# Attention softmax on one core: the exponentials' scale and VectorE's factor read from SBUF columns instead of constants

## The chip, the core and the metric

The kernel runs on one core of one Trainium2 chip. A core has a matrix engine (TensorE, "PE" in the profile; its weight loads are "PEld"), VectorE ("DVE"), ScalarE ("ACT"), GpSimd ("POOL") and a queue for transfers, SyncE ("SP"). They run side by side and meet at semaphores. The on-chip memories are SBUF, with 128 partitions, and PSUM, into which TensorE writes its results.

The metric is the device time of one execution in microseconds (us); smaller is better.

## What is computed

Attention over 32 heads with 2048 rows of 20 columns each, on normalised queries and keys, with one temperature for each head:

```python
def reference(q, k, v, t):
    eps = 1e-6
    qn = q / (jnp.sqrt((q * q).sum(axis=-1, keepdims=True)) + eps)
    kn = k / (jnp.sqrt((k * k).sum(axis=-1, keepdims=True)) + eps)
    logits = jnp.einsum('bhqd,bhkd->bhqk', qn, kn) * t[None, :, None, None]
    attn = _softmax(logits, axis=-1)
    return jnp.einsum('bhqk,bhkd->bhqd', attn, v)
```

The inputs are bf16 with B = 1, H = 32, S = 2048 and D = 640 / 32 = 20. The scores are bounded by the temperature, so the kernel takes no maximum away before the exponential. The sum of the weights comes out of the second product, from a column of ones beside v.

## The kernel before

For each head the 2048 x 2048 scores are cut into units of 128 keys by 512 queries. A unit's scores are one TensorE matmul (`qk_mm`, L837) of the transposed keys with the transposed queries, into a 512-column stretch of PSUM. Four such units side by side make a group, whose product with v (`pv_mm`, L857) is four matmuls that add into the PSUM tile `psO`.

Between the two products each score must become its exponential, and two engines share this work:

- **ScalarE** takes most of the units, in waves of two and three by turns (`WAVES`, `add_wave`, L905). A wave is one activation (L938) over 1024 or 1536 columns: it reads the scores in `psA`, takes the exponential and writes bf16 into the ring `p_ring`. `psA` has room for one wave of each size, so a wave's matmuls wait for the exponential two waves back.
- **VectorE** takes between 3 and 7 of a head's 16 groups (`DVE_TILES`, `add_dgroup`, L964). It reads the scores in `psD` (L998; called a read of scores below), multiplies them by `X_MUL`, adds `X_ADD` and writes int16 into `xt`. Read as a float16 number, that integer is an approximate exponential. Three shifted copies of it (L1008 on VectorE, or in pieces L1012 on GpSimd) and the plain one are each multiplied with a scaled v, and their sum averages the approximation's error. A read covers 1024 columns, or, where a group is in `SPLIT`, 512.

VectorE also prepares the heads to come: squares (L689), sums (L693), the inverse root (L697 to L718), the normalised rows (L735) and the scaled copies of v (L652). It finishes the heads that are done: transpose of `psO` (L870), reciprocal (L879) and product (L887). SyncE's queue loads q, k and v, transposes them by transfers and stores the results.

The order of the work on each engine is computed when the program is built. Each piece of work is a task with an engine, a planned duration, the tasks that it depends on and a priority. `list_schedule` (L118) plays these through time and writes down the order in which each engine takes them; it also chooses the form of the scores' matmuls and cuts GpSimd's pieces to fit beside VectorE's reads. `plan_waits` (L409) then turns the dependences into semaphore waits. A wait is left out where the engine is already known to have seen that count, directly or through a task that it waited for (L441 to L449). `emit` (L454) writes the instructions out. No order is changed while the kernel runs.

At the start VectorE fills constant tiles with memsets (L549), among them the task `z_one`, which fills `ones` with 1.0. TensorE's warm-up matmuls and GpSimd's identity matrix wait for it.

The scale of one other activation is a column in SBUF already: `qt0` (L776) multiplies the first head's queries by `t_f32[:, 0:1]`.

Of the kernel before, what the change touches and what calls it, by code (L numbers as in the profile page):

```python
# [12 lines left out]
F32 = mybir.dt.float32  # L13
# [3 lines left out]
ACT = mybir.ActivationFunctionType  # L17
# [12 lines left out]
X_MUL = 1024.0 * LOG2E  # L30
X_ADD = 1024.0 * (15.0 + math.log2(KEXP))
# [18 lines left out]
class Program:  # L50
# [31 lines left out]
    def add(self, eng, name, fn, dur, deps=(), pri=0.0, lat=0.0, dma=None):  # L82
        t = Task(eng, name, fn, dur, deps, pri, lat, dma)
        self.tasks.append(t)
        return t
# [379 lines left out]
def bass_standalone__qk_norm__prompt_kernel(  # L465
# [11 lines left out]
    WAVES = (2, 3)  # L477
# [27 lines left out]
    EXP0 = 0.063  # L505
# [4 lines left out]
    with ExitStack() as es:  # L510
# [6 lines left out]
        ones = sbuf("ones", [128, 512], BF16)  # L517
        ident = sbuf("ident", [128, 128], BF16)
        nil = sbuf("nil", [128, 32], BF16)
        qk_sb = sbuf("qk_sb", [128, NB * 2 * R, D], BF16)  # L520
        v_all = sbuf("vaug", [128, NV, R, 32], BF16)
        vaug = [v_all[:, i, :, :] for i in range(NV)]
# [25 lines left out]
        def memset(eng, ap, val, dur, pri):  # L548
            return add(eng, "z", lambda e, tk: e.memset(ap, val), dur, pri=pri)  # L549
# [38 lines left out]
        add("ACT", "warm", lambda e, tk: e.activation(act_scr[:, :], act_scr[:, :], ACT.Exp), 1.5, [scr0], -95)  # L588
        ld_t = dma("SP", "ld_t", tb16[:, :], bass.AP(t.tensor, 0, [[0, 128], [1, H]]), [], -40, "t")
        z_nil = memset("POOL", nil[:, :], 0.0, 0.1, -71)  # L590
        z_one = memset("DVE", ones[:, :], 1.0, 0.2, -99)
        z_lib = add("POOL", "lib", lambda e, tk: e.int64_add(
            ident[:, 0:4].bitcast(I64), ident[:, 4:8].bitcast(I64), 0), 0.2, [memset("POOL", ident[:, 4:8], 0.0, 0.1, -99.5)], -99.4)
        z_id = add("POOL", "id", lambda e, tk: e.affine_select(
# [310 lines left out]
        def add_wave(w):  # L905
            us = waves[w]
            slot = w % 2
            hs = sorted({A_units[i][0] for i in us})
            pair = next(([i, i + 1] for i in range(len(us) - 1)
                                          if A_units[us[i]][2] // 2 != A_units[us[i + 1]][2] // 2), [])  # L910
            parts = pair + [i for i in range(len(us)) if i not in pair]

            def f_qk(eng, rows):
                last = None
                for i in parts:
                    h, r, g = A_units[us[i]]
                    last = qk_mm(eng, h, r, g, psA[:, (slot * WAVES[0] + i) * 512:(slot * WAVES[0] + i + 1) * 512], rows)
                return last
            deps = [act.get(w - 2)]
            for h in hs:  # L920
                deps += qk_deps([A_units[u] for u in us if A_units[u][0] == h], w < EARLY_W)
            qk = add("PE", f"q3A{w}", lambda e, tk: f_qk(e, tk.rows), PE_MM, deps, w - 10000.0)
            if len(us) == 3 and LIGHT3:
                qk.modes = [("q3", 32, PE_MM + 0.01, 384.0), ("q2", 64, PE_MM * 2, 768.0)]
            elif len(us) == 3:
                qk.modes = [("q2", 64, PE_MM * 2, 768.0), ("qk", 128, PE_MM * 3, 1536.0)]
            else:
                qk.modes = [("q2", 64, PE_MM, 256.0 * len(us)), ("qk", 128, PE_MM * len(us), 512.0 * len(us)),
                            ("q3", 32, PE_MM, 128.0 * len(us))]
            if w < EARLY_W:  # L930
                qk.modes, qk.rows, qk.dur, qk.work = None, 32, PE_MM + 0.01, 128.0 * len(us)
            qks = [qk]
            for h in hs:
                qk_users[h] += qks
            p0 = us[0] % NP
            n = len(us) * 512
            war = [pv_of_group[(u - NP) // 4] for u in us if u >= NP]
            act[w] = add("ACT", f"exp{w}", lambda e, tk: e.activation(  # L938
                p_ring[:, p0 * 512:p0 * 512 + n], psA[:, slot * WAVES[0] * 512:slot * WAVES[0] * 512 + n], ACT.Exp),
                EXP0 + n / 1200.0, qks + war, w)  # L940

        def add_group(i):
            us = list(range(4 * i, 4 * i + 4))
# [20 lines left out]
        def add_dgroup(jg):  # L964
            js = D_groups[jg]
            sx = se = 0
            ox, oe = place(0, NX, len(js)), place(1, NE, len(js))
            bx, be = 2048 * ox, 2048 * oe
            w = 2048 * len(js)
            old = lambda n, i: last_use.get((n, (ox if n == "x" else oe) + i), [])  # L970
            new = {}
            t1s = []
            for i, j in enumerate(js):
                h, rg = D_tiles[j]
                due = h + (j - d0[h] + 0.3) / DVE_TILES[h] - DLEAD
                split = j in SPLIT
                for us in ((0, 1), (2,), (3,)) if split else ((0, 1), (2, 3)):
                    gs = [GORD[k] for k in us]
                    banks = [k % 2 for k in us]

                    def f_qk(eng, rows, h=h, rg=rg, gs=gs, banks=banks):
                        last = None
                        for g, bk in zip(gs, banks):
                            last = qk_mm(eng, h, rg[g], g, psD[:, 512 * bk:512 * bk + 512], rows)
                        return last
                    deps = [bank_t1.get(bk) for bk in banks] + (q0 if j < EARLY_D else [])
                    for g in gs:
                        deps += qk_deps([(h, rg[g], g)], j < EARLY_D)
                    qk = add("PE", f"qkD{j}.{us[0]}", lambda e, tk, f=f_qk: f(e, tk.rows), PE_MM, deps, due - 20000.0)
                    qk.modes = [("q2", 64, PE_MM, 256.0 * len(us)), ("qk", 128, PE_MM * len(us), 512.0 * len(us)),  # L990
                                ("q3", 32, PE_MM, 128.0 * len(us))]
                    if j < EARLY_D:
                        qk.modes, qk.rows, qk.dur, qk.work = None, 32, PE_MM + 0.01, 128.0 * len(us)
                    qk_users[h].append(qk)
                    for k0, m in [(k, 1) for k in us] if split else [(us[0], 2)]:
                        o = bx + 2048 * i + 512 * k0
                        c = 512 * (k0 % 2)
                        u = add("DVE", f"t1.{j}.{k0}", lambda e, tk, o=o, c=c, w=512 * m: e.tensor_scalar(  # L998
                            xt[sx][:, o:o + w], psD[:, c:c + w], X_MUL, X_ADD, ALU.mult, ALU.add),
                            0.067 + 512 * m / 960.0, [qk] + old("x", i), due - 5)  # L1000
                        for bk in range(k0 % 2, k0 % 2 + m):
                            bank_t1[bk] = u
                        t1s.append(u)
                t1_of[j] = t1s[-(4 if split else 2):]
            sh = []
            for i in range(len(PHASES)):
                dst, w = ss[i][0], 2048 * len(js)
                f = add("DVE", f"s{i}.{js[0]}", lambda e, tk, i=i, dst=dst: e.tensor_scalar(  # L1008
                    dst[:, be:be + w], xt[0][:, bx:bx + w], float(PHASES[i]), None, ALU.add), 0.068 + w / 3840.0,
                    t1s + [u for m in range(len(js)) for u in old(f"s{i}", m)], due)  # L1010
                if len(js) == 1 and jg >= 2:
                    f.alt = lambda c, n, i=i, dst=dst: lambda e, tk: e.int64_add(  # L1012
                        dst[:, be + 2 * c:be + 2 * (c + n)].bitcast(I64), xt[0][:, bx + 2 * c:bx + 2 * (c + n)].bitcast(I64),
                        PHASES[i] * LANES)
                    if chained.get(i) and ox and oe:
                        chained[i].next = f
                    chained[i] = f
                sh.append([(list(range(len(js))), f)])
            for m in range(len(js)):
                new["x", ox + m] = [u for us in sh for ms, u in us if m in ms]  # L1020
            for i, j in enumerate(js):
                h, rg = D_tiles[j]
                for nm, tile, dep, ph in [("x", xt[sx], t1_of[j], None)] + [
                        (f"s{n}", ss[n][se], [u for ms, u in sh[n] if i in ms], n) for n in range(len(PHASES))]:
                    p = add("PE", f"pv{nm}{j}", lambda e, tk, h=h, rg=rg, o=2048 * i + (bx if ph is None else be), tile=tile, ph=ph: pv_mm(
                        e, h, lambda g: rg[g],
                        lambda g: tile[:, o + 512 * GORD[g]:o + 512 * GORD[g] + 512].bitcast(FP16), ph),
                        PE_MM, dep + pv_base(h) + (vsc[h] if ph is not None else []), due + 0.2)
                    p.head = h
                    pv_users[h].append(p)  # L1030
                    new.setdefault((nm, (ox if nm == "x" else oe) + i), []).append(p)
            last_use.update(new)
# [76 lines left out]
```

## Time and profile before

| | us |
|---|---|
| median of 2 runs | 637.17 |
| the runs | 637.06 and 637.29 |
| the profiled execution | 638.55 |
| its span, first to last instruction | 636.8 |

The profile is of one execution. A line of its table of groups names the kernel's line, the engine, the operation, the tile written and the tile read with their shapes, and the count; then the group's busy time in us and the mean duration of one in ns; and last the engine's idle time just ahead of the group with what ended most of it. A line of the timeline begins with the start and the duration in us. A line of the windows view begins with the stretch and its length; then come the busy time of the asked instructions with their count, the granted TensorE clock (1.00 is full), the transfers' share and GB/s.

What belongs to the engines beside it:

| engine | busy us | share of the span | instructions |
|---|---|---|---|
| TensorE | 596.2 | 94% | 6267 |
| VectorE | 627.2 | 99% | 926 |
| ScalarE | 626.0 | 98% | 558 |
| GpSimd | 423.4 | 66% | 461 |

The granted TensorE clock was 1.000 over the span.

### The profile page before, as it was taken

How to read it: one execution, taken by the hardware profiler on the slowest of the kernel's cores; microseconds unless marked ns; L12 is line 12 of the kernel's file. 1: busy time of each engine (PE TensorE's matmuls, PEld its weight loads, DVE VectorE, ACT ScalarE, POOL GpSimd, SP SyncE). 2: the span in 40 equal slices, each digit the busy share in tenths (PEclk: the TensorE clock that was granted, in tenths of full speed). 3: DMA queues.
4: the chain of work that ended last, by engine and by line, in shares of the span. 5: the costliest groups of instructions: out<-in, count | busy, mean ns of one | idle time of the engine just before them, and what ended most of it. 6: DMA issues, size and time to landing. Idle time of an engine off the chain costs nothing.

```text
span 636.8 us, 15281 instructions
## 1 busy us (share of the span) xinstructions
PE 596.2 (94%) x6267; PEld 170.9 (27%) x6267; DVE 627.2 (99%) x926; ACT 626.0 (98%) x558; POOL 423.4 (66%) x461
## 2 busy tenths in 40 slices
PE   8898899999999989999999999999999999999997
PEld 2222222222222222222222222222222222222222
DVE  8999999999999999999999999999999999999997
ACT  7999999999999999999999999999999999999997
POOL 4265687777756787567776675777787777577443
PEclk9999999999999999999999999999999999999999
DMA  4554444333333313333323333433332241321100
GB/s 66 76 78 71 74 85 65 73 58 55 58 59 63 65 45 53 64 67 61 60 59 58 45 66 72 55 61 40 62 64 64 44 69 35 67 50 26 38 1 16
DMA packets 196917, 36.40 MB, mean 57 GB/s; under 512 B 172656, under 2 KB 196848, under 8 KB 196848
## 3 DMA queue, kind: packets, MB, share of 16 engines
q1 hardware_dynamic: 196656, 35.32, 33.3%
q8 instruction: 49, 0.80, 0.6%
q14 instruction: 20, 0.16, 0.1%
q10 hardware_dynamic: 192, 0.11, 0.1%
HBM read 7.87 MB, written 2.62 MB: 16 GB/s over the span
## 4 chain that ended last, share of the span: by engine, by line
ACT 88%; DVE 7%; PE 5%; issue 0%
ACT p_ring L938 88%; DVE xt L998 3%; PE psO L857 2%; DVE ss L1008 1%; PE psA L837 1%; PE psO L760 1%; PE psD L837 1%; DVE rs_sum L693 0%; DVE oT L870 0%; PE psO L802 0%; DVE sq L689 0%; DVE qkn L735 0%; DVE o_stage L887 0%; DVE vph L652 0%; DVE ones L549 0%
## 5 line engine op out<-in xcount | busy, mean ns | idle before, releaser
L938 ACT ACTIVATE p_ring<-psA 128x1024 bf16<-128x1024 f32 (+1 forms) x551 | 622.5, 1429 | 2.3 <-PE psA L837 2.3
L1012 POOL INT64_ADD ss<-xt x430 | 416.1, 972 | 200.3 <-DVE xt L998 51.9
L998 DVE TENSOR_SCALAR xt<-psD 128x1024 int16<-128x1024 f32 (+1 forms) x412 | 414.0, 1021 | 2.4 <-PE psD L837 1.8
L857 PE MATMUL psO<-ss,vph 128*32 128x512 f16 x2016 | 175.6, 385 | 0.0
L1008 DVE TENSOR_SCALAR ss<-xt 128x2048 int16<-128x2048 int16 x182 | 124.9, 688 | 0.6
L857 PE MATMUL psO<-p_ring,vaug 128*32 128x512 bf16 x1376 | 120.7, 384 | 0.0
L837 PE MATMUL psA<-qkT,kR 32*128 32x512 bf16 x619 | 109.4, 384 | 11.6 <-ACT p_ring L938 10.7
L837 PE MATMUL psA<-qz,kR 64*128 64x512 bf16 (+1 forms) x413 | 101.6, 385 | 5.6 <-ACT p_ring L938 5.1
L837 PE MATMUL psD<-qz,kR 64*128 64x512 bf16 (+1 forms) x359 | 97.7, 384 | 7.1 <-DVE xt L998 4.9
L837 PE MATMUL psA<-qkT 32*128 32x512 bf16 x220 | 67.1, 384 | 4.6 <-ACT p_ring L938 4.3
L857 PE MATMUL psO<-xt,vaug 128*32 128x512 f16 x672 | 66.5, 386 | 0.0
L857 PEld LDWEIGHTS psO<-ss,vph 128*32 128x32 f16 x2016 | 44.6, 94 | 74.6 <-issue 59.9
L837 PE MATMUL psD<-qz,qkT 64*128 64x512 bf16 (+1 forms) x123 | 46.5, 384 | 2.0 <-DVE xt L998 1.8
L837 PEld LDWEIGHTS psA<-qkT,kR 32*128 32x128 bf16 x619 | 26.3, 91 | 75.4 <-ACT p_ring L938 73.3
L857 PEld LDWEIGHTS psO<-p_ring,vaug 128*32 128x32 bf16 x1376 | 32.0, 94 | 52.3 <-issue 43.7
L837 PE MATMUL psA<-qz,qkT 64*128 64x512 bf16 (+1 forms) x124 | 43.2, 385 | 0.6 <-ACT p_ring L938 0.4
L837 PEld LDWEIGHTS psA<-qz,kR 64*128 64x128 bf16 (+1 forms) x413 | 24.4, 93 | 65.9 <-ACT p_ring L938 63.6
L837 PE MATMUL psD<-qkT,kR 32*128 32x512 bf16 x145 | 37.7, 382 | 3.2 <-DVE xt L998 2.3
L837 PEld LDWEIGHTS psD<-qz,kR 64*128 64x128 bf16 (+1 forms) x359 | 23.9, 93 | 57.9 <-DVE xt L998 50.4
L857 PEld LDWEIGHTS psO<-xt,vaug 128*32 128x32 bf16 x672 | 17.4, 94 | 31.0 <-issue 24.6
L735 DVE TENSOR_TENSOR qkn<-qk_sb,rs_r 128x640 bf16<-128x640 bf16 x31 | 25.3, 816 | 0.0
L693 DVE TENSOR_REDUCE rs_sum<-sq 128x32 f32<-128x640 bf16 x31 | 25.1, 810 | 0.0
(61 smaller groups left out, 201.0 us busy)
## 6 DMA issues: line engine op xcount, KB each, us to landing
kR<-qkT SPq DMA_DIRECT2D x62, 96.0 KB, 2.1
qz<-qkT SPq DMA_DIRECT2D x127, 32.0 KB, 1.8
kR<-qkT SPq DMA_DIRECT2D x62, 64.0 KB, 2.0
qk_sb<-in_k_dram SPq DMA_DIRECT2D x32, 80.0 KB, 3.0
vaug<-in_v_dram SPq DMA_DIRECT2D x32, 80.0 KB, 3.2
qk_sb<-in_q_dram SPq DMA_DIRECT2D x124, 20.0 KB, 2.5
out_dram<-o_stage SPq DMA_DIRECT2D x31, 80.0 KB, 1.9
kR<-qkT SPq DMA_DIRECT2D x62, 32.0 KB, 1.9
```

Source lines behind the costliest of these rows:

```text
L693: sums.append(dv("sum", lambda e, tk, i=i, k=k, src=src: e.tensor_reduce(rs["sum"][:, 2 * R * (i + k):2 * R * (i + k + 1)], src[:, 2 * R * ...
L735: norm[h] = [dv("norm", lambda e, tk, x=x, b=b, i=i: e.tensor_tensor(qkn[b][:, :, 0:D], x[:, :, :], bc(rs["r"][:, 2 * R * i:2 * R * (i + 1 ...
L760: warm.append(add("PE", "warm", lambda e, tk: e.matmul(psO[:, :], ones[:, 0:128], ones[:, :], start=True, stop=True), PE_MM, [z_one], -300))
L837: return eng.matmul(dst, lhsT, mov, tile_position=(p0, 0))
L857: last = eng.matmul(psO[32 * g:32 * g + 32, :], w, rhs_of(g), start=start, stop=False, skip_group_check=True, tile_position=(0, 32 * g))
L938: act[w] = add("ACT", f"exp{w}", lambda e, tk: e.activation(p_ring[:, p0 * 512:p0 * 512 + n], psA[:, slot * WAVES[0] * 512:slot * WAVES[0] ...
L998: u = add("DVE", f"t1.{j}.{k0}", lambda e, tk, o=o, c=c, w=512 * m: e.tensor_scalar(xt[sx][:, o:o + w], psD[:, c:c + w], X_MUL, X_ADD, ALU ...
L1008: f = add("DVE", f"s{i}.{js[0]}", lambda e, tk, i=i, dst=dst: e.tensor_scalar(dst[:, be:be + w], xt[0][:, bx:bx + w], float(PHASES[i]), No ...
L1012: f.alt = lambda c, n, i=i, dst=dst: lambda e, tk: e.int64_add(dst[:, be + 2 * c:be + 2 * (c + n)].bitcast(I64), xt[0][:, bx + 2 * c:bx + ...
```

## The change

A new tile `cols` of 128 x 2 float32 numbers lies in SBUF. Its first column is filled with 1.0 and its second with `X_MUL` by two memsets, in the same task as the memset of `ones` and ahead of it. Every exponential takes its scale from the first column, where before it had the constant 1.0. Every read of scores takes its factor from the second, where before it had the constant `X_MUL`; the addend `X_ADD` stays a constant. Both kinds of task now also depend on `z_one`. The numbers computed with are the same.

```diff
+        cols = sbuf("cols", [128, 2], F32)
...
-        z_one = memset("DVE", ones[:, :], 1.0, 0.2, -99)
+        z_one = add("DVE", "z", lambda e, tk: (e.memset(cols[:, 0:1], 1.0), e.memset(cols[:, 1:2], X_MUL),
+                                               e.memset(ones[:, :], 1.0))[2], 0.2, pri=-99)
...
             act[w] = add("ACT", f"exp{w}", lambda e, tk: e.activation(
-                p_ring[:, p0 * 512:p0 * 512 + n], psA[:, slot * WAVES[0] * 512:slot * WAVES[0] * 512 + n], ACT.Exp),
-                EXP0 + n / 1200.0, qks + war, w)
+                p_ring[:, p0 * 512:p0 * 512 + n], psA[:, slot * WAVES[0] * 512:slot * WAVES[0] * 512 + n], ACT.Exp, scale=cols[:, 0:1]),
+                EXP0 + n / 1200.0, qks + war + [z_one], w)
...
                         u = add("DVE", f"t1.{j}.{k0}", lambda e, tk, o=o, c=c, w=512 * m: e.tensor_scalar(
-                            xt[sx][:, o:o + w], psD[:, c:c + w], X_MUL, X_ADD, ALU.mult, ALU.add),
-                            0.067 + 512 * m / 960.0, [qk] + old("x", i), due - 5)
+                            xt[sx][:, o:o + w], psD[:, c:c + w], cols[:, 1:2], X_ADD, ALU.mult, ALU.add),
+                            0.067 + 512 * m / 960.0, [qk] + old("x", i) + [z_one], due - 5)
```

## The prediction

> **What bounds the kernel now.** I read the page first: busy shares, then the chain that ended last, then the costliest groups.
>
> ```profile
> span 636.8 us, 15281 instructions
> PE 596.2 (94%) x6267; PEld 170.9 (27%) x6267; DVE 627.2 (99%) x926; ACT 626.0 (98%) x558; POOL 423.4 (66%) x461
> ...
> ACT 88%; DVE 7%; PE 5%; issue 0%
> ...
> L938 ACT ACTIVATE p_ring<-psA 128x1024 bf16<-128x1024 f32 (+1 forms) x551 | 622.5, 1429 | 2.3 <-PE psA L837 2.3
> L1012 POOL INT64_ADD ss<-xt x430 | 416.1, 972 | 200.3 <-DVE xt L998 51.9
> L998 DVE TENSOR_SCALAR xt<-psD 128x1024 int16<-128x1024 f32 (+1 forms) x412 | 414.0, 1021 | 2.4 <-PE psD L837 1.8
> ```
>
> Two engines are full at once, ScalarE (98%) and VectorE (99%). The 551 exponentials alone fill 622.5 us and wait only 2.3 us in all. VectorE waits 2.4 us ahead of its 412 reads of scores. So nearly every nanosecond added to an exponential is added to the end; what is added to VectorE is added too, unless ScalarE has by then become slower by more. GpSimd (66%) has room. The change touches exactly these two groups, so the question is what a column operand costs in each.
>
> The groups kept apart by shape give durations:
>
> ```profile
> L938 ACT ACTIVATE p_ring<-psA 128x1536 bf16<-128x1536 f32 x275 | 451.2, 1641 | 1.6 <-PE psA L837 1.5
> L938 ACT ACTIVATE p_ring<-psA 128x1024 bf16<-128x1024 f32 x275 | 335.4, 1220 | 0.7 <-PE psA L837 0.7
> ...
> L938 ACT ACTIVATE p_ring<-psA 128x512 bf16<-128x512 f32 x1 | 0.6, 626 | 0.0
> L776 ACT ACTIVATE xq<-qk_sb,t_f 128x320 f32<-128x320 bf16 x1 | 0.6, 562 | 0.0
> L677 ACT ACTIVATE sq<-qk_sb 128x320 bf16<-128x320 bf16 x1 | 0.5, 469 | 0.2 <-DMA qk_sb<-in_q_dram 0.2
> L803 ACT ACTIVATE qkT<-psA 128x256 bf16<-128x256 f32 x1 | 0.4, 384 | 1.8 <-PE psA L794 1.8
> ...
> L606 ACT ACTIVATE t_f<-tb 128x32 f32<-128x32 bf16 x1 | 0.2, 228 | 0.5 <-DMA tb<-in_t_dram 0.5
> ```
>
> The row that decides most is L776: it is the one instruction of this kernel that already takes its scale from a column in SBUF. It took 562 ns for 320 columns; L677, with constants, took 469 ns for the same 320. The difference is 93 ns. The function and the output type differ too, so I check it against L606, a copy like L776 with a constant scale: from 32 to 320 columns with constants (228 to 469 ns) a column costs 0.837 ns, so L606's copy of 320 would take 469 ns, and L776 again stands 93 ns above. One column scale read by an activation that runs by itself costs 93 ns.
>
> Back to back, an activation costs less than alone:
>
> ```profile
> 302.23 1.61 ACT L938 ACTIVATE p_ring<-psA 128x1536 bf16<-128x1536 f32 x1
> 303.56 1.19 ACT L938 ACTIVATE p_ring<-psA 128x1024 bf16<-128x1024 f32 x1
> 304.46 1.63 ACT L938 ACTIVATE p_ring<-psA 128x1536 bf16<-128x1536 f32 x1
> ```
>
> The first ends at 303.84; the second starts 0.28 us before that. So the start in the record is the issue, not the beginning of the work, and a mean of 1429 ns includes waiting behind the one before. The real cost is 622.5 / 551 = 1130 ns. The columns (275 x 1536 + 275 x 1024 + 512 = 704,512) at 0.837 ns are 589.7 us; the other 32.8 us are about 60 ns for each exponential. Alone, the read from PSUM in L803 costs 384 - 256 x 0.837 = 170 ns beside its columns. So some 110 of 170 ns lie under the end of the one before, and 60 ns stay in the open, although the next one was issued 1429 - 1130 = 299 ns ahead on the mean.
>
> **The change part by part.**
>
> *Exponentials, 551 times, scale from a column.* Nothing else about them changes: same columns, same output, same order. No row shows a column scale back to back. Bounds: 93 ns each if the column is read only when the engine is done with the one before (551 x 93 = 51.2 us), and nothing if it is read in the 299 ns by which the instruction is issued early. Below nothing I see no way: no work goes away. I take 93. An operand issued 299 ns ahead ought to have been fetched long before, and yet 60 ns stay in the open with every exponential. That looks like a read that can't begin before the one before is done, and a column in SBUF is one more such read.
>
> [...]
>
> *Reads of scores, 412 times, factor from a column.*
>
> ```profile
> L998 DVE TENSOR_SCALAR xt<-psD 128x1024 int16<-128x1024 f32 x260 | 316.7, 1218 | 2.2 <-PE psD L837 1.8
> ...
> L998 DVE TENSOR_SCALAR xt<-psD 128x512 int16<-128x512 f32 x152 | 97.3, 685 | 0.2
> ```
>
> ```profile
> 108.15 1.22 DVE L998 TENSOR_SCALAR xt<-psD 128x1024 int16<-128x1024 f32 x1
> 109.29 0.82 DVE L735 TENSOR_TENSOR qkn<-qk_sb,rs_r 128x640 bf16<-128x640 bf16 x1
> 110.02 1.22 DVE L998 TENSOR_SCALAR xt<-psD 128x1024 int16<-128x1024 f32 x1
> ```
>
> A column costs (1218 - 685) / 512 = 1.041 ns, so 1024 of them are 1066 ns; from 108.15 to the next start pass 1140 ns, so about 70 ns stay open. No VectorE row of before has a column factor. Bounds: 0 and ScalarE's 93 ns. I take 70 ns, the row nearest to it (one opening of a read on VectorE itself): 412 x 70 = 28.8 us on VectorE; at 93 ns it would be 38.3 us. [...]
>
> *What of it counts.* The two engines work side by side, and the larger addition sets the end. By stretches, the 16 windows of 40 us; the one with the most reads of scores is this, first for L938, then for L998:
>
> ```profile
> 440.00:480.00 40.00, 40.00 (x37) 1.00 0.33 58
> ```
>
> ```profile
> 440.00:480.00 40.00, 29.31 (x37) 1.00 0.33 58
> ```
>
> ScalarE gets 37 x 93 = 3.4 us there and VectorE 37 x 70 = 2.6 us; in every other window VectorE's share is smaller still. So VectorE's 28.8 us lie beside ScalarE's 51.2 and cost nothing as long as ScalarE pays in full; without that cover they cost their 28.8. The TensorE order is fixed, so an exponential can still be kept waiting for its scores behind those of a late read of VectorE. I price that at 0, with up to a fifth of 28.8 us, 5.8, as upper end, since both engines run slack-free only over short stretches. On the other side up to 2.3 us of ScalarE's idle time may be absorbed.
>
> *Two more memsets at the start, on VectorE.*
>
> ```profile
> 0.88 0.09 DVE L549 MEMSET act_scr<- 128x32 f32 x1 [0.88 <-PEq L1094]
> 1.02 0.48 DVE L549 MEMSET ones<- 128x512 bf16 x1
> ...
> 2.28 0.91 DVE L549 MEMSET qz<- 128x1024 uint32 x1 [0.16 <-issue]
> 3.11 0.33 DVE L676 TENSOR_TENSOR sq<-qk_sb 128x320 bf16<-128x320 bf16 x1
> ```
>
> From the small memset to the next start pass 0.14 us; two cost 0 to 0.28. Behind them are queued the memset of ones (TensorE's warm-up waits for it), the other memsets and the first square, which starts without idle time, so I take 0.2 us. It delays the first exponential by no more than that.
>
> *The dependence on that task.* The order comes from planned durations, and those are unchanged (0.2 us for the task, the same for exponentials and reads). The task ends in the first 2 us, and every exponential and read already waits for a scores matmul that comes after it, so by the rule of L441 to L449 no wait is added: 0.
>
> **Sum.** The profiled execution: 638.55 us, span 636.8; 1.4 us above the median of 637.17. 638.55 + 51.2 + 0.2 = 690.0 by its own time. Against the median: 637.17 + 51.4 = 688.6 us.
>
> **The rivals.**
>
> *The columns cost nothing, the time stays.* The read of the column begins at issue. An exponential is issued 299 ns ahead of the end of the one before and needs 110 of them now; 110 + 93 = 203 still fits. For VectorE it takes that the column comes along with the stream. For it: the 299 ns. Against it: the 60 ns that being early doesn't remove, and a VectorE start that is only 1220 - 1140 = 80 ns ahead. Time: 637.17 + 0.2 = 637.4. It decides as soon as less than 12.7 / 551 = 23 ns is left for each exponential and less than 12.7 / 412 = 31 ns for each read (12.7 us is 2%).
>
> [...]
>
> *ScalarE hides it, VectorE pays.* The same 299 ns, against 80 ns on VectorE. Then VectorE sets the end: 637.4 + 28.8 = 666, between 637 and 676 for 0 to 93 ns.
>
> *ScalarE pays in part.* If half of the 93 ns goes under the 110: 637.4 + 25.6 = 663 from ScalarE, and VectorE's 28.8 then decides: 666 again.
>
> *The column read collides with GpSimd.* L1012's 430 adds run beside the reads of scores. If a column read of VectorE had to wait for SBUF behind a running add, half of 972 ns for, say, half of the 412 reads would be 100 us: 738. It takes more than 51.2 / 412 = 124 ns for each read to overtake ScalarE. Against it: the reads write SBUF beside these adds today and keep to 1218 ns.
>
> **How the numbers follow.** Forecast (ScalarE pays in full) 0.53, at 688.6; its own range is 684 (ScalarE pays 85 ns a time: 637.4 + 46.8) to 695 (688.6 + 5.8). Nothing changes: 0.21. VectorE alone or ScalarE in part: 0.20. Collision: 0.06. The range from 637 to 695 leaves out the collision and the edges. Faster by over 2% (about what a measurement of this kernel can tell from no change): 0.01, since no part removes work. Within 2%: 0.21 from the first rival and 0.02 from the low end of the second, 0.23. Slower: 0.76.
>
> **What would show it.** In the changed profile, busy time of L938 over 551: near 1223 ns if right, 1130 if the columns are free. L998's 1024-wide form: near 1290 ns if VectorE pays 70, 1218 if not. ScalarE should stay at 98% and VectorE fall to about (627 + 29) / 688 = 95%, with idle time ahead of L998 released by TensorE. Wrong would be: L938 at 1130 with the time grown, L998 above 1340, or idle time ahead of L938 of more than some 8 us.

## The result, and the profile after

The changed kernel takes 686.36 us (two runs, 685.68 and 687.03) where the kernel before takes 637.17: a ratio of 1.0772 (95% interval 1.0725 to 1.0818), 49.2 us more. The forecast was 688.6.

The page of the changed kernel (its exponentials and reads of scores stand two lines further down, at L940 and L1000; the profiled execution took 685.68 us, and the records of 17 of its 6267 matmuls are missing):

```profile
span 683.9 us, 15266 instructions
PE 611.7 (89%) x6250; PEld 170.1 (25%) x6267; DVE 661.7 (97%) x928; ACT 674.5 (99%) x558; POOL 422.1 (62%) x461
...
ACT 97%; PE 2%; DVE 0%; issue 0%
...
L940 ACT ACTIVATE p_ring<-psA,cols 128x1024 bf16<-128x1024 f32 (+1 forms) x551 | 670.9, 1664 | 1.1 <-PE psA L839 1.1
L1014 POOL INT64_ADD ss<-xt x430 | 414.8, 969 | 248.0 <-DVE xt L1000 77.8
L1000 DVE TENSOR_SCALAR xt<-psD,cols 128x1024 int16<-128x1024 f32 (+1 forms) x412 | 438.8, 1083 | 14.4 <-PE psD L839 7.5
```

ScalarE's exponentials are the chain now (97%, before 88%). Their busy time rose from 622.5 to 670.9 us: 48.4 us, 88 ns for each of 551. The medians differ by 49.2 us and the spans of the two profiled executions by 47.1, so the exponentials are the whole loss as far as two runs can tell. VectorE, which was as full as ScalarE before, has idle time ahead of its reads of scores: 14.4 us, before 2.4.

The reads by shape, from the groups kept apart by shape:

```profile
L1000 DVE TENSOR_SCALAR xt<-psD,cols 128x1024 int16<-128x1024 f32 x260 | 332.8, 1280 | 12.8 <-PE psD L839 7.1
...
L1000 DVE TENSOR_SCALAR xt<-psD,cols 128x512 int16<-128x512 f32 x152 | 106.0, 745 | 1.6 <-PE psD L839 0.4
```

Both widths are about 60 ns longer (1280 against 1218, 745 against 685). The cost goes with the instruction, not with its columns; the price of a column of scores, (1280 - 745) / 512 = 1.045 ns, is what it was.

In order of time (timeline of VectorE in the changed kernel; start, duration):

```profile
114.47 1.28 DVE L1000 TENSOR_SCALAR xt<-psD,cols 128x1024 int16<-128x1024 f32 x1
115.67 0.82 DVE L737 TENSOR_TENSOR qkn<-qk_sb,rs_r 128x640 bf16<-128x640 bf16 x1
116.40 1.28 DVE L1000 TENSOR_SCALAR xt<-psD,cols 128x1024 int16<-128x1024 f32 x1
117.59 0.68 DVE L1010 TENSOR_SCALAR ss<-xt 128x2048 int16<-128x2048 int16 x1
```

From 114.47 to the next start pass 1.20 us, before 1.14. The next instruction still starts 0.08 us before the read's end (115.75): the overlap is what it was, and the column's time lies in the open.

The exponentials in order of time (timeline of ScalarE in the changed kernel; start, duration):

```profile
321.35 1.84 ACT L940 ACTIVATE p_ring<-psA,cols 128x1536 bf16<-128x1536 f32 x1
322.77 1.42 ACT L940 ACTIVATE p_ring<-psA,cols 128x1024 bf16<-128x1024 f32 x1
323.77 1.86 ACT L940 ACTIVATE p_ring<-psA,cols 128x1536 bf16<-128x1536 f32 x1
325.19 1.44 ACT L940 ACTIVATE p_ring<-psA,cols 128x1024 bf16<-128x1024 f32 x1
```

The second starts at 322.77, 0.42 us before the first ends (323.19), and ends at 324.19, 1.00 us after it. Its 1024 columns at 0.837 ns are 0.86 us of that. So it was issued at least 0.42 us ahead, and still some 0.14 us lie in the open between one stream and the next. From one end to the next a 1536-wide exponential takes 1432 ns and a 1024-wide one 1005 (medians of the trace), so a column costs 427 / 512 = 0.834 ns. Less the columns, 151 ns stay open in the median, where it was 63. It is 151 or 152 whether the record of the exponential begins 0.2 or 0.5 us ahead. Being early hides nothing of the column.

### The profile page after: what moved, and what is told of

Same layout as the page of the kernel before. It is cut to its first block, busy times and chain, and to the rows that moved or that the text cites. A ratio compares the mean times of both kernels' runs of the same rounds, so it can differ in the third digit from the quotient of the medians.

```text
span 683.9 us, 15266 instructions
## 1 busy us (share of the span) xinstructions
PE 611.7 (89%) x6250; PEld 170.1 (25%) x6267; DVE 661.7 (97%) x928; ACT 674.5 (99%) x558; POOL 422.1 (62%) x461
## 4 chain that ended last, share of the span: by engine, by line
ACT 97%; PE 2%; DVE 0%; issue 0%
ACT p_ring L940 97%; PE psO L762 1%; PE psO L859 0%; PE psA L839 0%; DVE oT L872 0%; PE psO L769 0%; PE psD L839 0%; DVE ones L593 0%; DVE o_stage L889 0%; PE psO L804 0%; PE psA L796 0%; PE psD L796 0%; DVE rec L881 0%; DVE act_scr L550 0%; DVE cols L592 0%
## 5 line engine op out<-in xcount | busy, mean ns | idle before, releaser
L940 ACT ACTIVATE p_ring<-psA,cols 128x1024 bf16<-128x1024 f32 (+1 forms) x551 | 670.9, 1664 | 1.1 <-PE psA L839 1.1
L1000 DVE TENSOR_SCALAR xt<-psD,cols 128x1024 int16<-128x1024 f32 (+1 forms) x412 | 438.8, 1083 | 14.4 <-PE psD L839 7.5
L839 PE MATMUL psA<-qz,kR 64*128 64x512 bf16 (+1 forms) x406 | 99.7, 387 | 17.9 <-ACT p_ring L940 11.0
L839 PE MATMUL psD<-qz,kR 64*128 64x512 bf16 x351 | 94.9, 385 | 2.4 <-DVE xt L1000 2.1
L839 PEld LDWEIGHTS psA<-qkT 32*128 32x128 bf16 x220 | 15.8, 90 | 38.3 <-ACT p_ring L940 37.7
```

The costliest lines, as they stand in the source:

```text
L839: return eng.matmul(dst, lhsT, mov, tile_position=(p0, 0))
L940: act[w] = add("ACT", f"exp{w}", lambda e, tk: e.activation(p_ring[:, p0 * 512:p0 * 512 + n], psA[:, slot * WAVES[0] * 512:slot * WAVES[0] ...
```

## The experiments

Beside the first four runs the kernel before took 638.38 us, and beside the last four 638.63. So differences to it are read rather than times.

| run | column operands | us | ratio to before, 95% interval |
|---|---|---|---|
| ctrl | none | 638.86 | 1.0011 (1.0001 to 1.0022) |
| act_only | scale of exponentials | 685.40 | 1.0736 (1.0720 to 1.0752) |
| dve_only | factor of reads | 655.13 | 1.0264 (1.0248 to 1.0279) |
| act_wide | scale of the 1536-wide exponentials | 659.49 | 1.0333 (1.0315 to 1.0350) |
| act_two | scale and bias of exponentials | 736.90 | 1.1532 (1.1509 to 1.1555) |
| dve_two | factor and addend of reads | 680.97 | 1.0657 (1.0634 to 1.0680) |
| replan | as the change, other planned durations | 692.51 | 1.0840 (1.0824 to 1.0857) |
| rebal | as replan, six groups moved | 705.90 | 1.1050 (1.1032 to 1.1069) |

### Is it the operand? (ctrl)

From the changed kernel, both operands back to constants; tile, memsets and dependences stay:

```diff
-... ACT.Exp, scale=cols[:, 0:1]),
+... ACT.Exp),
-... psD[:, c:c + w], cols[:, 1:2], X_ADD, ALU.mult, ALU.add),
+... psD[:, c:c + w], X_MUL, X_ADD, ALU.mult, ALU.add),
```

> Tile, memsets and dependences of the change stay; exponentials and reads of scores take constants again. Theory A (the column operand itself costs: about 88 ns of each exponential and 60 ns of each read, and the engine with the larger sum sets the end): 637.2 + at most 0.3 = 637 to 638 us. Rival B (the two memsets or the added dependences cost): 650 to 686 us.

The two groups of ctrl's page:

```profile
L940 ACT ACTIVATE p_ring<-psA 128x1024 bf16<-128x1024 f32 (+1 forms) x551 | 622.8, 1432 | 2.6 <-PE psA L839 2.4
L1000 DVE TENSOR_SCALAR xt<-psD 128x1024 int16<-128x1024 f32 (+1 forms) x412 | 413.2, 1019 | 2.8 <-PE psD L839 2.1
```

They are back at 622.8 and 413.2 us (before 622.5 and 414.0). 638.86 us is 0.5 us over the kernel before, at the edge of what can be told. Everything else of the change costs next to nothing, so Rival B falls. In the traces the order on every engine and all waits are the same as before, apart from the two memsets.

### ScalarE alone (act_only)

```diff
-... psD[:, c:c + w], cols[:, 1:2], X_ADD, ALU.mult, ALU.add),
+... psD[:, c:c + w], X_MUL, X_ADD, ALU.mult, ALU.add),
```

> Column scale in the exponentials, constant factor in VectorE's reads. Theory A: ScalarE alone sets the end, 637.2 + 551 x 0.088 = 685.7 us, the same as with both. Rival C (the two additions add up in part, because a late read of scores keeps an exponential waiting): clearly faster than with both, below 683 us.

685.4 us, as with both columns: the intervals of the ratios (1.0720 to 1.0752, and 1.0725 to 1.0818) overlap. From the page of act_only:

```profile
L940 ACT ACTIVATE p_ring<-psA,cols 128x1024 bf16<-128x1024 f32 (+1 forms) x551 | 670.9, 1667 | 1.0 <-PE psA L839 1.0
L1000 DVE TENSOR_SCALAR xt<-psD 128x1024 int16<-128x1024 f32 (+1 forms) x412 | 416.0, 1024 | 32.6 <-PE psD L839 23.9
```

The exponentials' busy time is 670.9 us with and without the column on VectorE. VectorE's idle time ahead of its reads is 32.6 us here and 14.4 with both columns: the column on VectorE went into idle time. Rival C falls.

### VectorE alone (dve_only)

```diff
-... ACT.Exp, scale=cols[:, 0:1]),
+... ACT.Exp),
```

> Column factor in VectorE's reads, constants in the exponentials. Theory A: VectorE now sets the end and its cover is gone, 637.2 + 412 x 0.060 = 662 us; L1000's 1024-wide form at 1280 ns as with both, ScalarE idle by about 25 us more. Rival D (VectorE's reads had room, its 99% being partly waiting): 637 to 648 us. Rival C: more than 668 us, since each engine's lateness reaches the other through TensorE's fixed order.

655.13 us, 16.8 us more: between A (24.7 more) and D (none to 11). VectorE does set the end now; of the page of dve_only:

```profile
PE 601.9 (92%) x6267; PEld 165.1 (25%) x6267; DVE 645.4 (99%) x928; ACT 635.9 (97%) x558; POOL 425.8 (65%) x461
...
DVE 92%; PE 5%; issue 2%; DVEq 0%
...
L940 ACT ACTIVATE p_ring<-psA 128x1024 bf16<-128x1024 f32 (+1 forms) x551 | 632.4, 1252 | 8.7 <-PE psA L839 6.0
L1000 DVE TENSOR_SCALAR xt<-psD,cols 128x1024 int16<-128x1024 f32 (+1 forms) x412 | 435.1, 1076 | 0.5 <-PE psD L839 0.4
```

The chain is VectorE's (92%), and its wait ahead of the reads is down to 0.5 us. Rival C's 668 us and more didn't come. But VectorE's busy time rose by 18 us (627.2 before), not by the 24.7 that 412 columns of 60 ns cost. The rest went into waits that the profile counts as busy: two VectorE instructions overlap by some 80 ns in the record, so a read whose scores come less than 80 ns late shows no idle time, only a shorter overlap. Over all 412 reads of the kernel before, the time from the end of the instruction before to the read's own end adds up to 394 us in the trace; the columns of scores are 358, which leaves 87 ns for each read, though the median read has 67. Here the mean is 128 and the median 127. So some 8 us of the kernel before were waits ahead of the reads, and a slower VectorE no longer has them: 2.4 us of them stood as idle time, the other 6 in the busy time. They are waits for scores: in the trace of before, 98 reads overlap the instruction ahead of them by less than 70 ns or not at all, and each of these begins some 24 ns after a matmul of scores has signalled its end.

ScalarE's waits show only in part too. Its idle time ahead of the exponentials rose by 6.4 us (from 2.3 to 8.7), and their busy time by 9.9 (from 622.5 to 632.4) for the same work.

### Every second exponential (act_wide)

```diff
-... psD[:, c:c + w], cols[:, 1:2], X_ADD, ALU.mult, ALU.add),
+... psD[:, c:c + w], X_MUL, X_ADD, ALU.mult, ALU.add),
...
-... ACT.Exp, scale=cols[:, 0:1]),
+... ACT.Exp, scale=cols[:, 0:1] if n == 1536 else 1.0),
```

> Column scale in the 275 exponentials of 1536 columns alone, constants in the others and on VectorE. Theory A (the read of the column waits for the end of the instruction before, whatever that one's operands are): 637.2 + 275 x 0.088 = 661.5 us; a 1536-wide one ends 1280 + 151 ns after the one before, a 1024-wide one 853 + 63. Rival E (only one place for a column value, so that it can be fetched ahead only when the one before holds none): every second one hides it, 637 to 641 us. Rival F (the cost comes when the operand is put back, in the one behind): same time as A, but the 1024-wide ones carry the 88 ns.

659.49 us, 21.1 us more: A's 24.3 less some 3. The timeline of ScalarE in act_wide:

```profile
299.61 1.62 ACT L940 ACTIVATE p_ring<-psA,cols 128x1536 bf16<-128x1536 f32 x1
301.04 1.11 ACT L940 ACTIVATE p_ring<-psA 128x1024 bf16<-128x1024 f32 x1
301.94 1.64 ACT L940 ACTIVATE p_ring<-psA,cols 128x1536 bf16<-128x1536 f32 x1
```

The ends are at 301.23, 302.15 and 303.58. The 1024-wide one, without a column, ends 0.92 us after the one before it; the 1536-wide one 1.43 us. Less their columns (0.86 and 1.29 us at 0.837 ns) that leaves 0.06 and 0.14 us; over all of them, at 0.834 ns, the medians are 60 and 151 ns. The instruction with the column carries the cost, though the one before it holds no column. So Rivals E and F fall. Of the 3 us missing, 0.8 are the 60 ns in place of 63 (275 times); another 1.6 are the idle time ahead of the 1536-wide ones, which the kernel before had and this one hasn't. The rest, under 1 us, is no more than such runs can tell.

### Two columns (act_two and dve_two)

act_two, with the constant factor on VectorE and a third column, filled with 0.0, in a `cols` that is now four wide:

```diff
-... ACT.Exp, scale=cols[:, 0:1]),
+... ACT.Exp, scale=cols[:, 0:1], bias=cols[:, 2:3]),
```

> Exponentials with two columns, the scale and a bias of 0.0; VectorE with constants. Theory A1 (each column is a read of its own, one after the other): 151 + 88 = 239 ns open for each exponential, 685.4 + 551 x 0.088 = 734 us. Rival A2 (both columns come with one read): 151 ns open, 685 us.

dve_two, with the constant scale on ScalarE and the third column filled with `X_ADD`:

```diff
-... psD[:, c:c + w], cols[:, 1:2], X_ADD, ALU.mult, ALU.add),
+... psD[:, c:c + w], cols[:, 1:2], cols[:, 2:3], ALU.mult, ALU.add),
```

> VectorE's reads of scores with two columns, factor and addend; the exponentials with constants. Theory A1 (a read for each column): 125 + 60 = 185 ns open for each read of scores, 655 + 412 x 0.060 = 680 us. Rival A2 (one read for both): 125 ns open, 655 us.

736.9 and 680.97 us: near A1's 734 and 680 both times. Each column is paid for by itself. From the pages, act_two's exponentials and dve_two's reads:

```profile
L940 ACT ACTIVATE p_ring<-psA,cols 128x1024 bf16<-128x1024 f32 (+1 forms) x551 | 721.1, 1714 | 2.4 <-PE psA L839 2.4
```

```profile
L1000 DVE TENSOR_SCALAR xt<-psD,cols 128x1024 int16<-128x1024 f32 (+1 forms) x412 | 461.9, 1142 | 2.6 <-PE psD L839 2.5
```

The exponentials' busy time grows by 48.4 us with the first column and by 50.2 with the second (721.1 - 670.9): 88 and 91 ns. On VectorE the median open time of a 1024-wide read is 67, 127 and 187 ns with none, one and two. The second column there costs 680.97 - 655.13 = 25.8 us, 63 ns for each of 412 reads: full price, as it should be where dve_only has already used up the short waits.

### Is it the order? (replan and rebal)

replan plans with the measured durations:

```diff
-    EXP0 = 0.063
+    EXP0 = 0.151
...
-                            0.067 + 512 * m / 960.0, [qk] + old("x", i) + [z_one], due - 5)
+                            0.127 + 512 * m / 960.0, [qk] + old("x", i) + [z_one], due - 5)
```

> The changed kernel, with the planned durations set to what was measured: 0.151 us beside the columns of an exponential in place of 0.063, and 0.127 in place of 0.067 for a read of scores. The plan's order on all engines follows from that. Theory A (ScalarE is full, so an order can't win back what each exponential costs): 684 to 690 us. Rival G (the loss comes from an order planned for other durations): 650 to 680 us.

rebal has replan's durations and adds one group to VectorE's in six heads:

```diff
-    DVE_TILES = [4, 4, 4, 7, 3, 6, 6, 5, 5, 6, 4, 5, 6, 6, 5, 6, 5, 4, 6, 6, 6, 3, 6, 5, 4, 6, 5, 7, 5, 6, 6, 6]
+    DVE_TILES = [4, 4, 5, 7, 4, 6, 6, 5, 5, 6, 5, 5, 6, 6, 5, 6, 5, 5, 6, 6, 6, 4, 6, 5, 5, 6, 5, 7, 5, 6, 6, 6]
```

> As replan, and six groups more are given to VectorE (one more in heads 2, 4, 10, 17, 21 and 24; 174 in place of 168). Each group takes four units of 427 ns and their share of 0.151, together 1.95 us, from ScalarE, 11.7 us for six, and adds about 3.0 us to VectorE, 18 us, which had 19 us idle. Theory A: 686.4 - 11.7 = 675 us. Rival G: no gain beside replan, or a loss, since VectorE's idle time lies in pieces that can't be used.

692.51 and 705.90 us: both are slower than the change itself, and both miss theory A's range. Of the groups by shape, the shifted copies on VectorE in replan and in rebal:

```profile
L1010 DVE TENSOR_SCALAR ss<-xt 128x2048 int16<-128x2048 int16 x218 | 147.2, 686 | 2.0
```

```profile
L1010 DVE TENSOR_SCALAR ss<-xt 128x2048 int16<-128x2048 int16 x222 | 151.0, 687 | 1.9
```

The new plans leave fewer copies to GpSimd: VectorE makes 218 and 222 where it made 182, which are 22 and 26 us more of its time. The end of replan, from the timelines of ScalarE and of VectorE:

```profile
668.93 12.25 ACT L940 ACTIVATE p_ring<-psA,cols 128x1536 bf16<-128x1536 f32 x10
```

```profile
682.13 0.70 DVE L1010 TENSOR_SCALAR ss<-xt 128x2048 int16<-128x2048 int16 x1
682.74 1.28 DVE L1000 TENSOR_SCALAR xt<-psD,cols 128x1024 int16<-128x1024 f32 x1
...
684.53 1.28 DVE L1000 TENSOR_SCALAR xt<-psD,cols 128x1024 int16<-128x1024 f32 x1
685.84 1.90 DVE L1010 TENSOR_SCALAR ss<-xt 128x2048 int16<-128x2048 int16 x3
...
689.29 0.49 DVE L889 TENSOR_TENSOR o_stage<-oT,rec 128x320 bf16<-128x320 f32 x1
```

The last exponential ends at 681.2 us of the span, in the change at 679.5. VectorE still has two reads of scores to do after that, and ends 8.6 us after the last exponential; in the change it ends 2.3 us after. These two differences, 1.7 and 6.3 us, are together the 7.9 us by which the spans differ, but for rounding. That the additional copies are what made VectorE late is argued, not shown: no run moved the copies alone.

In rebal the tail is longer. The last row of ScalarE and the last of VectorE:

```profile
669.59 12.33 ACT L940 ACTIVATE p_ring<-psA,cols 128x1536 bf16<-128x1536 f32 x10
```

```profile
701.10 0.49 DVE L889 TENSOR_TENSOR o_stage<-oT,rec 128x320 bf16<-128x320 f32 x1
```

The last exponential ends at 681.9 us, and VectorE 19.7 us after it, with eight reads of scores still to begin. With six groups more the end is VectorE's. In replan the exponentials themselves are what they were in the change; their groups on the pages of replan and rebal:

```profile
L940 ACT ACTIVATE p_ring<-psA,cols 128x1024 bf16<-128x1024 f32 (+1 forms) x551 | 671.4, 1561 | 2.4 <-PE psA L839 1.7
```

```profile
L940 ACT ACTIVATE p_ring<-psA,cols 128x1024 bf16<-128x1024 f32 (+1 forms) x541 | 660.4, 1510 | 14.3 <-PE psO L859 13.2
```

So these two orders win back nothing of what the columns cost, and the gain that Rival G expected of replan doesn't show. In rebal the loss is what Rival G expected; whether for its reason, that VectorE's idle time lies in unusable pieces, is not shown. Theory A's ranges were missed because I took the rest of the plan as given. In rebal ScalarE waited 14.3 us ahead of its exponentials as well, 13.2 of them for room in the ring that a second product hadn't yet read (`psO`), which is more than the 11.7 us of work taken from it. These two plans say nothing on what a plan made with as much care for these durations could reach; that stays open.

## Why the prediction was right, and where it was off

**The price on ScalarE** (taken at 93 ns, 51.2 us) was the step that decided. It measured 88 ns back to back, 48.4 us. The row of the one activation that already had a column scale gave the size. That none of it would be hidden was a guess by likeness: 60 ns stayed open however early an exponential was issued (62 or 63 in the median, with its record beginning from 0.1 to 0.4 us ahead), so a column might stay open too. No row of before showed it; the changed kernel and act_wide do, with 151 ns open in the median where there is a column. The check of the 93 ns against L606 could not have failed, since the 0.837 ns had been worked out from that same row and L677. The size held all the same: an exponential alone takes 89 ns more with the column (below), and a column of scores costs it 0.834 ns, against the 0.837 from L606 and L677. That the read of a column can't begin before the instruction before is done was my reading of the 60 ns. The 151 ns, at 0.2 and at 0.5 us of lead alike, agree with it; when the column is read, no trace shows.

**The rival that the columns are free** fell with act_only (685.4 us) and act_wide (659.49 us). Exponentials that begin only after the one before has ended show the cost of one alone, here a row of before and one of the change:

```profile
62.72 1.45 ACT L938 ACTIVATE p_ring<-psA 128x1536 bf16<-128x1536 f32 x1 [1.51 <-PE psA L837]
```

```profile
24.36 1.54 ACT L940 ACTIVATE p_ring<-psA,cols 128x1536 bf16<-128x1536 f32 x1 [0.33 <-PE psA L839]
```

In the trace they took 1452 and 1541 ns. Less 1536 columns at 0.834 ns that is 171 ns without a column scale and 260 with one; back to back 63 and 151 stay open. So some 108 ns lie under the recorded end of the one before in both cases, and the column adds nothing to them. The rival that half of the column is hidden there fell with that.

**The price on VectorE** (taken at 70 ns, 28.8 us) measured 60 ns, 24.7 us. The 70 ns were those of another thing, what stays open with a read whose operands are constants, so that they came near was luck. That it would lie beside ScalarE's was right: act_only and the change agree, and the upper end for exponentials kept waiting (5.8 us) wasn't needed.

**"What is added to VectorE is added too"** was too strong. With ScalarE's cover gone, the rival in which VectorE alone pays was put at 666 us. dve_only gave 655. That is an addition of 16.8 us in place of 28.8. Some 4 us of the difference are the price (60 ns, not 70). The other 8 are the failed step, that VectorE was taken as full: it had 2.4 us of idle time ahead of its reads and some 6 us of waits within its 99%, hidden by the 80 ns overlap. For the same reason VectorE's share after was 97% and not the 95% forecast: its busy time grew by 34.5 us, of which the columns are 24.7, so some of its new waiting is recorded as busy.

**The start and the waits.** 0.2 us for two memsets and none for dependences: ctrl measured 0.5 us for both, barely over its uncertainty (0.1 to 1.4 us).

**The collision with GpSimd** didn't happen: its adds took 969 ns (before 972), and the reads gained the same 60 ns at both widths.

## What to carry to other kernels

A per-partition column in place of a constant cost a fixed time here for each instruction and each column: 88 ns on ScalarE, where 151 ns stayed open in the median at 1024 and at 1536 columns, and 60 ns on VectorE, at 512 and at 1024. On ScalarE neither early issue (151 ns at 0.2 and at 0.5 us of lead) nor a neighbour without columns (151 ns in act_wide) hid it. For an estimate, multiply it by the count of instructions on the engine that sets the end: 551 x 88 ns = 48.5 us, and 49.2 were measured. Where the value is the same in all partitions, as both were here, it belongs in the instruction. Where it is not, fewer and wider instructions should pay less, an estimate from the same price at both widths; no run changed their number. To know how full an engine is, compare the distance between successive ends with the work in between: a busy share of 99% held some 6 us of waits here. On ScalarE the only constant that was run is 1.0; whether another would cost the same is not shown.

## What the runs showed that was not expected

The columns add up one by one: 63, 151 and 242 ns in the open on ScalarE with none, one and two, and 67, 127 and 187 ns on VectorE. The second costs about what the first does (91 and 88 ns on ScalarE, 60 and 60 on VectorE), although they lay in one tile, on VectorE side by side. Why a column's time isn't hidden under the instruction before is not shown by any of these runs; they show only that it adds its 88 or 60 ns to what stays open.
